# First layer norm of a fused attention and feed-forward kernel: two statistics split into tasks, the first transposed tile copied out by two engines, and another written-out order

## The chip, the cores and the metric

The kernel runs on one core of a Trainium2 chip. The metric is the device time of one launch in microseconds (us). Five engines work side by side: TensorE (PE: matmuls, with its weight loads shown as PEld), VectorE (DVE), ScalarE (ACT), GpSimd (POOL) and SyncE (SP, which here only issues transfers). Each engine takes its instructions in the order in which they stand in its queue; what crosses engines is tied by semaphores.

## The reference, cut to what matters

```
xn  = (x - mean(x)) / sqrt(var(x) + 1e-5)          # x: 2048 x 512, per row
q, k, v = xn @ wq, xn @ wk, xn @ wv                # 32 heads of 16
for s in 4 segments of 512 rows:
    p      = softmax(q_s k_s^T / 4 + mask)         # causal inside the segment
    a_dot  = p v_s
    a_mem  = phi(q_s) M / (phi(q_s) z + 1e-6)      # phi(t) = t+1 if t>0 else exp(t)
    o_s    = g * a_mem + (1 - g) * a_dot           # g = sigmoid(beta), per head
    M, z  += phi(k_s)^T v_s, sum phi(k_s)
out = x + o @ wo + silu(xn @ w1) @ w2              # w1: 512 x 1792, w2: 1792 x 512
```

Inputs and output are bf16. The layer norm is needed by every product, so nothing but warm-up matmuls can run on PE before the first rows are normed.

## The kernel before, in words

The 2048 rows are 16 tiles of 128 rows, four tiles to a segment. The layer norm of a segment (function `ln`) works tile by tile: DVE takes statistics (`bn_stats`, then `bn_aggr`, line 583 and 584; in segment 0 also an addition of epsilon, line 586), POOL raises the variance to the power -1/2 (`rstd`, lines 596 and 606), DVE norms (`xn`, line 617). In segments 1 to 3 the normed tile is transposed by a transfer (`xnT`, line 651, issued on SP). In segment 0 PE transposes it against an identity into a PSUM bank (`tr`, line 630) and one engine copies the bank out into `xnT` (line 643 on ACT for tiles 0 to 2, line 645 on DVE for tile 3). Tile 2 of segment 0 has its statistics on ACT instead.

From the four transposed tiles PE makes keys and queries in blocks of eight heads (four units `u` to a segment), values, and the feed-forward's hidden tiles (`h`: a matmul group, then a tanh on ACT at line 1174 and a product on DVE at line 1178, `glu`). For the very first unit keys and queries are made in pieces: `k0` for tile 0, for tile 1, and for tiles 2 and 3 together, and `q0` the same. A product of scores `S` (line 504, into the four PSUM banks `psS`) is followed by an exponential on ACT (line 870, 1.88 us each, 72 of them) and two causal masks on POOL (line 889). `PV` multiplies the probabilities with the values into two PSUM banks, which DVE copies out into `N` and `O` (line 958). PE has four banks `ps` beside `psS`; a group that finds none free waits for the copy that frees one. One constant is worked out on the way: the heads' gate `gcol` from a load of `beta` (`bet`, 128 partitions x 64 bytes), which the attention's end in segment 0 needs first.

No queue is left to chance. The program first makes some 1700 tasks, each with its engine and its instructions, and then emits them in the sequence of `ORDER`, a list of task numbers written into the file; that list alone says how tasks follow each other on each engine. Buffers are handed out in the same sequence. A task's own waits are those of its data and buffers only: the planner's durations and due times that stand beside the tasks set nothing on the chip.

At the head of the program SP and ACT issue the loads: the four tiles of segment 0, then `w_v`, half of `w_k`, half of `w_q` (ACT), half of `w_1`, tiles 4 to 7, and the other halves. Before that data is there PE runs 52 small matmuls on the identity (`warm`).

Of the kernel before, what the change touches and what calls it, by code (L numbers as in the profile page):

```python
# [10 lines left out]
BF16 = mybir.dt.bfloat16  # L11
# [3 lines left out]
P = 128  # L15
S = 2048
D = 512
# [47 lines left out]
1 3 5 6 14 27 0 53 28 29 17 15 54 2 30 31 32 63 33 34 35 36 58 37 38 18 39 40 41 55 4 64 65  # L65
42 43 44 45 46 47 48 59 60 56 7 49 50 51 61 70 52 66 67 57 114 71 115 62 116 117 68 69 97 72
8 118 96 73 74 109 100 16 98 110 111 9 101 102 104 10 11 99 103 112 113 105 119 21 120 121
122 184 185 136 137 268 138 269 139 270 123 271 26 75 76 77 304 305 188 272 84 129 130 131
132 189 187 140 143 106 141 306 12 13 273 307 147 148 133 149 150 192 193 124 125 126 127 151
107 78 79 80 142 274 128 152 83 195 275 308 153 276 108 85 86 154 196 197 309 89 179 180 181  # L70
182 191 277 198 278 155 156 163 164 279 165 166 167 200 201 194 186 286 287 288 289 183 290
87 280 281 135 282 283 291 134 298 299 203 204 202 81 168 169 170 171 292 88 172 284 199 190
205 206 300 301 293 294 295 302 285 208 303 296 158 220 144 209 210 159 160 207 297 328 346
347 222 348 349 350 212 213 221 82 310 311 312 329 313 330 90 363 364 365 366 351 145 146 314
331 161 162 367 315 332 174 157 333 91 211 19 216 433 20 434 435 436 437 316 317 318 319 382
383 384 217 219 368 385 386 214 226 352 353 443 444 445 215 446 447 322 320 321 323 324 325
354 369 218 227 230 175 173 326 355 390 391 327 392 393 176 356 357 223 394 396 224 231 234
358 428 429 225 430 431 359 360 361 387 677 678 679 680 177 178 432 420 421 235 238 422 423
424 334 335 336 337 681 239 229 371 682 372 373 374 242 340 395 338 409 410 411 412 339 237
341 241 233 236 438 375 342 240 243 245 343 344 244 439 228 413 388 92 246 247 451 452 453  # L80
454 455 456 457 458 459 460 461 462 463 464 465 466 440 232 441 401 248 345 415 22 442 402
403 250 517 467 518 404 405 378 379 93 519 94 579 468 520 262 251 254 406 263 521 264 252 580
253 689 425 690 691 692 522 255 380 256 257 426 572 362 249 671 672 673 571 674 693 258 694
407 259 675 676 523 524 525 526 527 528 261 529 530 531 487 488 260 587 381 683 389 489 490
491 492 493 370 494 495 581 582 585 586 408 573 574 588 496 591 583 265 684 685 377 686 497
416 23 592 595 267 498 687 707 266 708 376 709 710 688 502 503 589 448 450 596 504 593 711
712 598 597 505 506 599 507 508 499 532 427 533 509 510 500 577 511 501 469 512 600 603 872
513 24 594 590 397 604 449 701 534 702 470 601 703 704 705 873 575 706 584 535 514 607 515
516 536 471 537 538 602 606 605 623 476 25 477 578 624 608 625 475 611 417 612 614 613 539
540 541 542 713 714 715 716 576 841 842 473 717 718 615 616 1115 874 1116 843 875 844 845  # L90
1117 1118 1119 609 610 474 755 756 757 617 758 759 619 620 543 544 545 785 719 720 786 721
722 478 876 629 1120 546 723 1103 1104 724 787 788 472 725 877 726 483 1105 789 727 1106 618
728 622 630 633 1107 485 621 626 486 479 480 1108 398 399 737 634 627 738 739 761 740 484 637
481 635 846 847 848 628 731 732 733 734 878 883 729 730 636 849 482 547 632 548 414 638 640
641 850 549 741 735 736 418 760 742 885 565 566 550 551 567 568 400 553 554 555 419 556 569
642 884 645 644 762 695 696 793 794 795 796 697 797 646 647 648 790 698 812 552 813 649 557
814 815 831 631 643 816 832 650 881 833 834 835 699 700 639 559 560 561 562 563 763 764 653
654 766 767 886 768 769 819 665 666 657 836 837 838 770 839 743 652 744 95 658 1006 745 746
840 747 748 879 749 750 661 662 751 774 775 998 791 776 777 778 804 667 805 656 752 660 806
753 807 655 820 754 798 1013 823 824 663 825 826 827 808 913 659 914 915 958 959 1005 960  # L100
1014 1017 1018 997 651 664 668 670 669 817 780 1016 961 962 851 963 779 964 887 1133 1007
1008 1009 1010 999 1021 1022 1000 1134 1097 792 1098 1099 888 880 1100 1003 1011 893 1135
1136 1137 916 917 918 1025 1026 1138 1024 965 966 967 1019 1012 968 852 919 1101 854 855 856
857 858 859 860 861 862 863 864 865 866 867 868 869 1029 1015 920 921 922 870 928 929 821 923
924 1001 1023 818 889 894 969 1028 930 931 765 1027 1102 1030 1033 1034 970 925 971 932 926
892 933 934 935 936 1031 937 1037 1032 938 939 927 1020 1109 1110 1111 972 1112 1038 891 1004
1113 1049 1041 940 1114 895 941 1002 1050 1127 1128 1051 1129 1130 942 799 896 882 1035 1188
1036 1189 1190 1191 558 781 1042 1039 1131 890 782 783 1045 1196 1197 1132 1044 1198 1199 897
1151 1200 1152 1153 1040 1043 1154 1181 1182 1183 1184 1046 1192 898 1055 1241 1155 1156 1185
899 1047 1242 1243 1244 1048 900 1056 1201 1052 1059 901 1245 902 1053 903 564 784 904 909  # L110
809 1246 1247 1248 1249 943 1251 771 1250 905 1060 828 944 1187 945 1252 772 1202 1063 810
946 1054 947 1121 1186 1122 1123 906 1124 822 1064 1125 1256 1257 1258 1259 1062 1061 910
1260 811 1067 1126 948 1253 1254 1203 1204 1205 1206 1207 1065 1255 949 950 951 1068 1071 829
1057 830 952 953 853 907 908 1211 1212 954 955 956 1213 911 773 912 1072 1075 1282 1283 1214
1284 1208 1218 1219 1220 1221 1058 1222 1070 1073 1285 800 1226 1215 1227 1228 1229 957 1076
1079 1139 1140 1141 1066 1069 1230 1142 1074 1091 801 802 1080 1092 1143 1083 1084 1157 1158
1159 1160 570 1082 973 974 975 976 1161 1077 1093 1286 1145 1146 1087 1209 977 1088 1162 1147
1287 1148 991 992 1144 993 994 871 1232 985 986 1288 1295 987 988 989 990 1149 1150 1407 1408
1085 995 1163 1164 1165 1166 1233 1234 1235 1289 1167 1291 1236 979 980 1411 1412 981 1168
982 1237 983 803 1169 1170 1171 1172 1086 1078 1090 1173 1089 1410 1193 1081 1094 1095 1216  # L120
1096 1415 1175 1409 1176 1296 1177 1523 1178 1524 1525 1526 1290 1264 1265 1266 1416 1297
1267 1268 1269 1419 1270 1174 1210 1179 1493 1180 1494 1271 1298 1299 1495 1420 1496 1272
1194 1497 1262 1498 1273 1417 1413 1261 1274 1414 1275 1276 1277 1418 1217 1278 1279 1353
1354 1355 1303 1302 1423 1280 1195 1356 1293 1357 1358 1424 1359 1360 1304 1305 1306 1426
1338 1339 1340 1361 1527 1528 1362 1427 1511 1512 1513 1514 1428 1363 1341 1342 1422 1301
1343 1344 1515 1421 1345 1431 1432 1346 1364 1430 1311 1365 1516 1347 1300 1366 1425 1443
1367 1445 1435 1436 1517 1518 1519 1520 1315 1348 1444 1349 1292 1323 1521 1434 1294 1324
1312 1307 1433 1325 1326 1522 1437 1439 1440 1327 1328 1329 1313 1350 1308 1351 1429 1223
1316 1309 1438 1352 1314 1442 1441 1330 1263 1331 1332 1310 1238 1449 1450 1451 1333 1317
1318 1319 996 1334 1335 1336 978 1337 1446 1447 1448 1239 1240 1320 1453 1454 1368 1452 1456  # L130
1535 1536 1537 1499 1500 1501 1502 1503 1538 1539 1231 1540 1224 1369 1370 1457 1321 1371
1372 1373 1374 1504 1553 1554 1555 1375 1225 1556 1458 1461 1462 1577 1322 1578 1579 1459
1455 1383 1384 1460 1385 1557 1463 1386 1387 1464 1505 1506 1507 1580 1508 1465 1466 1376
1377 1395 1396 1397 1509 1398 1378 1399 1379 1380 1558 1381 1469 1470 1510 1541 1468 1542
1543 1467 1382 1544 1485 1473 1388 1545 1559 1581 1486 1560 1561 1562 1582 1583 1529 1530
1531 1532 1487 1474 1476 1592 1593 1563 1389 1390 1400 1475 1477 1546 1590 1564 1533 1594
1534 1281 1571 1572 1573 1574 1586 1595 1391 1392 1471 1393 1394 1478 1401 1547 1548 1588
1549 1480 1550 1402 1575 1551 1481 1482 1565 1403 1552 1479 1472 1591 1483 1484 1576 1566
1567 1568 1569 1657 1584 1599 1600 1404 1405 1658 1659 1660 1621 1622 1639 1614 1623 1624
# [113 lines left out]
def kernel(  # L253
# [292 lines left out]
    def ln(s, due):  # L546
        first = s == 0
        for js in LNG if first else ((0, 1), (2, 3)):
            ag = []
            for j in js:  # L550
# [41 lines left out]
                if first and j == STJ:  # L592
                    ag[-1].ready = STR
# [819 lines left out]
```

## Time and profile before

| what | value |
|---|---|
| median of 13 runs | 228.8 us (227.71 to 230.65) |
| profiled execution | 229.2 us, of which the profile's span is 227.5 us |
| PE busy | 218.5 us (96%), 2800 matmuls |
| ACT, DVE, POOL busy | 181.5, 172.6, 160.9 us |
| first half of `w_k` used by PE | from 9.92 us |
| first half of `w_q` used by PE | from 12.51 us |
| first exponential starts | 16.91 us |
| mean granted PE clock | 0.992 |

The span runs from the first instruction to the last; the 1.7 us between it and the profiled execution's own time lie around it. Busy times are unions of an engine's instructions. In the timeline a row gives the start, the length, the engine, the line, the operation with output and input, how many instructions are merged, and in brackets the idle time before and what ended it.

### The profile page before, as it was taken

Reading aid. Unit: us, or ns where it says so; the run is one execution under the profiler, and the core shown is the slowest. Engines: PE = TensorE matmul, PEld = TensorE weight load, DVE = VectorE, ACT = ScalarE, POOL = GpSimd, SP = SyncE. Lnnn points to the kernel's source line nnn. Section 1 sums busy time; section 2 is a strip of 40 time slices with the busy share of each in tenths; the row PEclk is TensorE's granted clock in tenths of the full one; section 3 lists DMA queues with packets and bytes.
Section 4 is the critical chain, followed back from the end, with each engine's and each line's share of the span. In section 5 each row is a group of like instructions: output and inputs, shape, how many; then the busy total and the mean of one; then the engine's idle time right before and its main releaser. Section 6 shows DMA issues by size and latency. Waiting matters only on the chain.

```text
span 227.5 us, 6765 instructions
## 1 busy us (share of the span) xinstructions
PE 218.5 (96%) x2800; PEld 104.0 (46%) x2800; DVE 172.6 (76%) x307; ACT 181.5 (80%) x166; POOL 160.9 (71%) x281
## 2 busy tenths in 40 slices
PE   7689999999998999999999999999999999999994
PEld 7444444354543353534444445435454544445553
DVE  3649889687798667888897599898656697676883
ACT  4339999999998989999978889889998798994200
POOL 3705678999999756779899777866985976469300
PEclk9969999999999999999999999999999999999999
DMA  6980462708414532143026642001406220123402
GB/s 176 356 256 0 94 121 33 179 6 261 133 23 96 102 71 82 62 105 125 1 57 134 77 139 63 0 12 43 118 15 159 87 70 0 50 65 113 129 8 92
DMA packets 30851, 21.10 MB, mean 93 GB/s; under 512 B 15972, under 2 KB 29924, under 8 KB 30820
## 3 DMA queue, kind: packets, MB, share of 16 engines
q1 hardware_dynamic: 29476, 19.88, 33.8%
q10 hardware_dynamic: 1344, 0.79, 1.1%
q8 instruction: 22, 0.36, 0.7%
q14 instruction: 9, 0.07, 0.1%
HBM read 11.73 MB, written 2.64 MB: 63 GB/s over the span
## 4 chain that ended last, share of the span: by engine, by line
PE 77%; DVE 6%; POOL 5%; DMA 5%; ACT 3%; issue 2%; ACTq 1%; POOLq 0%
PE ps L504 65%; PE psS L504 12%; DMA w_q<-in_A_wq_dram 5%; ACT Pt L870 2%; POOL Pt L889 2%; DVE xn L617 2%; POOL rstd L606 1%; POOL kB L747 1%; DVE hT L1178 1%; POOL pq L675 1%; DVE st L583 1%; DVE O L958 1%; DVE pq L681 1%; DVE kT L742 1%; POOL rstd L596 0%
## 5 line engine op out<-in xcount | busy, mean ns | idle before, releaser
L870 ACT ACTIVATE Pt<-psS 128x2048 bf16<-128x2048 f32 x72 | 135.2, 1877 | 17.0 <-PE psS L504 14.9
L889 POOL TENSOR_SCALAR_AFFINE_SELECT Pt<-Pt 64x512 bf16<-64x512 bf16 (+1 forms) x144 | 89.2, 628 | 27.0 <-ACT Pt L870 22.0
L504 PE MATMUL ps<-xnT,w 128*128 128x512 bf16 x224 | 59.5, 380 | 1.3 <-DVE O L958 0.8
L504 PE MATMUL ps<-w,hT 128*128 128x512 bf16 (+1 forms) x210 | 52.9, 366 | 0.0
L1178 DVE SCALAR_TENSOR_TENSOR hT<-hT,ps 128x512 bf16<-128x512 bf16 x56 | 37.3, 678 | 15.7 <-ACT hT L1174 15.3
L1174 ACT ACTIVATE hT<-ps 128x512 bf16<-128x512 f32 x56 | 32.6, 596 | 0.5 <-PE ps L504 0.2
L504 PEld LDWEIGHTS <-hT 128*128 128x128 bf16 x238 | 21.7, 98 | 23.9 <-issue 3.1
L504 PEld LDWEIGHTS <-w 128*128 128x128 bf16 x224 | 20.4, 98 | 25.3 <-issue 3.8
L504 PE MATMUL psS<-qT,kB 32*128 32x256 bf16 (+5 forms) x640 | 28.6, 261 | 0.1
L504 PEld LDWEIGHTS <-kB 32*128 32x128 bf16 x640 | 11.8, 92 | 26.3 <-issue 24.2
L747 POOL TENSOR_SCALAR kB<-kT,pm 128x512 bf16<-128x512 bf16 x30 | 22.3, 749 | 0.9
L504 PE MATMUL ps<-xnT,w_q 128*128 128x512 bf16 (+2 forms) x72 | 18.2, 372 | 1.7 <-DMA w_q<-in_A_wq_dram 1.7
L504 PE MATMUL ps<-xnT,w_k 128*128 128x512 bf16 (+2 forms) x72 | 18.6, 364 | 1.2 <-DMA w_k<-in_A_wk_dram 1.2
L504 PE MATMUL ps<-Pt,V 64*32 64x256 bf16 (+5 forms) x640 | 19.8, 260 | 0.0
L504 PE MATMUL ps<-Pt,VS 64*32 64x256 bf16 (+5 forms) x640 | 18.7, 261 | 0.0
L504 PE MATMUL ps<-w_v,xnT 128*128 128x512 bf16 x64 | 18.2, 390 | 0.3 <-DMA w_v<-in_A_wv_dram 0.3
L504 PEld LDWEIGHTS <-V 64*32 64x32 bf16 x640 | 14.2, 91 | 8.3 <-issue 3.6
L504 PE MATMUL ps<-w_o,N 128*128 128x512 bf16 (+1 forms) x57 | 14.8, 368 | 0.0
L807 DVE CAST V<-ps 128x512 bf16<-128x512 f32 x16 | 11.0, 685 | 4.5 <-PE ps L504 4.2
L1080 POOL TENSOR_TENSOR pq<-pq,Dr 128x512 bf16<-128x512 bf16 x12 | 14.2, 1189 | 0.2
L583 DVE BATCH_NORM_STATS2 st<-x_all 128x6 f32<-128x512 bf16 x15 | 10.2, 679 | 4.3 <-DMA x_all<-in_A_x_dram 4.3
L504 PEld LDWEIGHTS <-VS 64*32 64x32 bf16 x640 | 12.8, 91 | 0.2
(105 smaller groups left out, 254.5 us busy)
## 6 DMA issues: line engine op xcount, KB each, us to landing
w<-in_B_w_dram SPq DMA_DIRECT2D x4, 896.0 KB
VS<-V SPq DMA_DIRECT2D x8, 264.0 KB
R<-dR SPq DMA_DIRECT2D x15, 128.0 KB
out_dram<-o_t SPq DMA_DIRECT2D x15, 128.0 KB
Dr<-dE SPq DMA_DIRECT2D x12, 128.0 KB
x_all<-in_A_x_dram SPq DMA_DIRECT2D x2, 512.0 KB
N<-O SPq DMA_DIRECT2D x12, 64.0 KB
w_v<-in_A_wv_dram SPq DMA_DIRECT2D x1, 512.0 KB
```

The lines of the kernel that those rows point to most:

```text
L504: nc.tensor.matmul(o, lhsT=l, rhs=r, start=start, stop=stop, **k)
L583: nc.vector.bn_stats(out=b.tile[:], in_=xt(t))
L606: nc.gpsimd.tensor_tensor(out=rs, in0=mv[:, t : t + n, 1:2] if first else rs, in1=lnc[:, 0:n, 1:2], op=ALU.pow,)
L617: nc.vector.tensor_scalar(out=xb.tile[:], in0=xt(t), scalar1=mv[:, t, 0:1], scalar2=rstd[:, t, 0:1], op0=ALU.subtract, op1=ALU.mult,)
L675: nc.gpsimd.tensor_scalar(out=dst_b.tile[:], in0=dst_b.tile[:], scalar1=1.0, scalar2=0.0, op0=ALU.min, op1=ALU.max,)
L747: nc.gpsimd.tensor_scalar(out=kB[u].tile[:, :, KB * r : KB * r + KB], in0=kT[u].tile[:].rearrange("p (a b) -> p a b", b=KB), scalar1=pm[:, ...
L807: nc.vector.tensor_copy(out=bass_pair(o), in_=i)
L870: nc.scalar.activation(out=pb.tile[:], in_=psS[:], func=AF.Exp, scale=SCALE)
L889: nc.gpsimd.affine_select(out=v, in_=v, compare_op=ALU.is_ge, fill=0.0, base=0, pattern=pat, channel_multiplier=-1,)
L1080: nc.gpsimd.tensor_tensor(out=pb.tile[:], in0=pb.tile[:], in1=rb.tile[:], op=ALU.mult)
L1174: nc.scalar.activation(out=hb.tile[:], in_=b.tile[:], func=AF.Tanh, scale=0.5)
L1178: nc.vector.scalar_tensor_tensor(out=hb.tile[:], in0=hb.tile[:], scalar=1.0, in1=b.tile[:], op0=ALU.add, op1=ALU.mult)
```

## The change

It has three parts in the code and one in the list.

1. The statistics of tiles 1 and 3 of segment 0 are two tasks instead of one: `bn_stats`, and then `bn_aggr` with the addition of epsilon. The instructions are the same.
2. The transposed tile 0 is copied out of its bank by ACT (two of four column blocks) and DVE (the other two). All products of segment 0 that read a transposed tile through `first_tile` or `v_tile` also wait for that second half.
3. `ORDER` is another list, for 1724 tasks in place of 1721.

```
-ORDER = """ 1 3 5 6 14 27 0 53 28 29 17 15 54 2 30 31 ...   (1721 numbers)
+ORDER = """ 1 3 5 6 0 53 15 2 65 14 27 28 29 30 31 32 ...   (1724 numbers)
...
+    extra = []
...
-                def f_st(t=t, b=b, vj=vj):
+                cut = first and j in (1, 3)
+
+                def f_st(t=t, b=b):
                     nc.vector.bn_stats(out=b.tile[:], in_=xt(t))
+
+                def f_ag(t=t, b=b, vj=vj):
                     nc.vector.bn_aggr(out=mv[:, t, :], in_=b.tile[:])
                     if first:
                         nc.vector.tensor_scalar(
                             out=vj, in0=vj, scalar1=EPS, scalar2=None, op0=ALU.add
                         )
...
-                    eng = "DVE" if j == 3 else "ACT"
...
+                    parts_ = (("ACT", 0, 2), ("DVE", 2, 2)) if j == 0 else (
+                        ("DVE" if j == 3 else "ACT", 0, 4),)
+                    for eng, lo, n_ in parts_:
+                        def f_e(j=j, pb=pb, eng=eng, lo=lo, n_=n_):
+                            o = xnT_b[0].tile[:, lo : lo + n_, j * P : (j + 1) * P]
+                            i = pb.tile[:].bitcast(BF16)[:, lo * P : (lo + n_) * P].rearrange(
+                                "p (a b) -> p a b", a=n_)
...
-            pcs.append(A("PE", ..., [xnT_done[0][j] for j in js] + [loads],
+            pcs.append(A("PE", ..., [xnT_done[0][j] for j in js] + extra + [loads],
...
-                     lambda ki: w_v[:, ki, :], (xnT_done[s] if s else [xnT_done[0][j]]) + [ld_v], ...
+                     lambda ki: w_v[:, ki, :], (xnT_done[s] if s else [xnT_done[0][j]] + extra) + [ld_v], ...
```

The new list changes the sequence on every engine but ACT's transfer queue, from the first POOL instruction to the last transfer. The stretches that the prediction speaks of, with the tiles' numbers (`v00` is the values of tile 0, `N3` and `O3` are the copies of line 958 for unit 3, `rstd 8,9` the two POOL instructions for tiles 8 and 9; "tiles 8 to 11" is one load):

| queue, stretch | before | changed |
|---|---|---|
| PE, head | 22 warm pairs, tr0, 3 warm, tr1, 1 warm, v00, tr2, k0 tile 1, k0 tile 0, tr3, q0 tile 0, q0 tile 1, k0 tiles 2-3, q0 tiles 2-3, v01, S0 | 20 warm pairs, tr0, 2 warm, tr1, 2 warm, k0 tile 0, v00, tr2, k0 tile 1, 1 warm, tr3, 1 warm, q0 tile 0, q0 tile 1, q0 tiles 2-3, a quarter of v03, k0 tiles 2-3, S0 |
| DVE, head | statistics 0, 1, xn0, xn1, statistics 3, xn2, xn3, V0, xnT3 | statistics 0, 1 (both tasks), xn0, xn1, half of xnT0, statistics 3 (both tasks), xn2, xn3, kT, xnT3 |
| DVE, norm of tiles 8-11 | statistics 10, 11, 9, 8, then two glu, acc, phi, phi, xn11, phi, xn10, gsum, O3, N3 | statistics 9, 8, 10, phi, xn8, xn9, glu, M32, statistics 11, acc, phi, O3, N3, gcol, phi, phi, xn10 |
| DVE, norm of tiles 12-15 | statistics, O7, N7, xn14, phi, xn13, xn15 | statistics 15, qT, glu, xn14, xn15, glu, O7, N7, phi, xn13 |
| SP, after the head | xnT4, phiK, VS, VS, xnT6, xnT5, xnT7, phiK, phiK, half of w_2, phiK (unit 3), half of w_2, w_o, tiles 8 to 11 | xnT4, VS, VS, phiK, xnT6, xnT7, `bet`, xnT5, phiK, phiK, phiK (unit 3), both halves of w_2, w_o, tiles 8 to 11 |
| SP, load of `bet` | last of the loads at the head | see the row above |
| DVE, end | the copy `mem` (line 1242) stands ahead of the last unit's PV copies | `mem` stands right ahead of the two `tailA` (lines 1260 and 1264) |

## Prediction

> **What bounds the kernel now.** I read the page first, then PE's waits, then the head in the windows view, then the two stretches where PE waits, in the timeline. The page says that PE has work nearly all the time, and that its clock is lowered once, near the start:
>
> ```profile
> PE 218.5 (96%) x2800; PEld 104.0 (46%) x2800; DVE 172.6 (76%) x307; ACT 181.5 (80%) x166; POOL 160.9 (71%) x281
> ...
> PEclk9969999999999999999999999999999999999999
> ```
>
> Busy matmul rows can hide bubbles, so I checked the spacing: eight matmuls of 512 columns take 1.89 us in one row, and one alone shows 0.38, so (1.89 - 0.38) / 7 = 0.216 us from start to start, with no room in it. The waits of PE between 16 and 224 us name only three:
>
> ```profile
> PE ps L504 <- DVE O L958: 0.8, 1, 0.8
> PE ps L504 <- DVE hT L1178: 0.3, 1, 0.3
> PE ps L504 <- DVE kT L742: 0.2, 1, 0.2
> ```
>
> So from the moment PE has its operands the time is PE's work plus small holes. Moving a PE task earlier or later gains nothing in itself. Only three things can change the time: when dense work starts, at which clock it runs, and the holes. The head, as rows of the windows view (PE busy second, granted clock second from the right of the engines):
>
> ```profile
> 5.84:9.26 3.42, 2.60 (x29) 1.71 (x26) 2.63 (x9) 1.66 (x3) 2.21 (x13) 1.00 1.04 362
> 9.26:12.67 3.41, 1.00 (x15) 0.84 (x16) 0.93 (x3) 0.58 (x2) 2.33 (x13) 1.00 1.10 362
> 12.67:16.08 3.41, 3.41 (x19) 2.22 (x18) 1.63 (x4) 1.38 (x3) 0.00 (x0) 0.50 0.94 276
> ```
>
> After a stretch with 1.00 us of work PE gets half its clock for 3.41 us, just when it is dense: 1.7 us lost. What it was short of is in the timeline, weights:
>
> ```profile
> 7.49 1.02 PE L504 MATMUL ps<-w_v,xnT 128*128 128x512 bf16 x4 [0.30 <-DMA w_v<-in_A_wv_dram]
> ...
> 9.92 0.62 PE L504 MATMUL ps<-xnT,w_k 128*128 128x128 bf16 x8 [1.18 <-DMA w_k<-in_A_wk_dram]
> ...
> 12.51 0.93 PE L504 MATMUL ps<-xnT,w_q 128*128 128x128 bf16 x8 [1.74 <-DMA w_q<-in_A_wq_dram]
> ```
>
> The holes of 0.3 and 0.8 us lie in the norm of tiles 8 to 11. DVE waits for those tiles' load, then for POOL's `rstd`, and the copy that frees PE's bank stands behind the `xn`:
>
> ```profile
> 59.39 0.69 DVE L583 BATCH_NORM_STATS2 st<-x_all 128x6 f32<-128x512 bf16 x1 [0.95 <-DMA x_all<-in_A_x_dram]
> ...
> 68.55 0.41 DVE L617 TENSOR_SCALAR xn<-x_all,mv,rstd 128x512 bf16<-128x512 bf16 x1 [0.60 <-POOL rstd L606]
> ...
> 70.42 0.68 DVE L958 CAST O<-ps 128x512 bf16<-128x512 f32 x1
> ```
>
> [...]
>
> **The change part by part**, against the profiled execution (229.2 us; it is 0.4 above the median of 228.8, so its loss of clock is somewhat above the usual one).
>
> *Split statistics.* The second task stands directly behind the first on DVE for tile 1 and tile 3. The same instructions come in the same sequence: 0.
>
> *Copy of tile 0 in two halves.* ACT's copy is 0.6 us (1.31 for two). Its half should take 0.37, as line 779's copy of 256 columns, and DVE's half at most 0.42, which is what the row of 512 columns at line 645 took. DVE does it after xn1 (ends 6.62), so tile 0 is whole at 6.9 to 7.1 instead of 7.0. Nobody can use the gain: PE's next task is then `k0` of tile 0, which waits for `w_k` until 9.92. DVE's statistics of tile 3 slip by up to 0.42; its transpose ran only at 10.38, although xn3 ended at 8.84, 1.5 us of cover. 0, from -0.1 to +0.1.
>
> *PE's head.* `k0` of tile 0 now stands ahead of v00 and tr2, so PE idles from about 7.2 (end of tr1 and its warm pairs) to 9.92. Between 9.92 and 12.51 it must then do v00 (4 x 0.216 = 0.86), eight small `k0` (8 x 0.056 = 0.45, 128 of 512 columns being a quarter of 0.216), two transposed tiles (8 x 0.056 = 0.45) and two warm pairs (0.22): 2.0 us in 2.6, so at full clock nothing slips past 12.51. All that stood ahead of `w_q` before still does.
>
> *Clock.* The new hole moves the poor stretch forward. In 5.84 to 9.26 PE would hold some 16 to 20 small matmuls, about 1.3 us of busy rows, as poor as the 1.00 that brought on half clock. With the same phase the slow 3.41 us would then be 9.26 to 12.67[...]. Of the 2.0 us of work 1.4 is done by 12.67 (2.75 us at half rate), the rest by 13.3: 0.8 lost in place of 1.7. I take -0.9 in this phase. Ends: -1.7 (not lowered) and 0 (the phase puts the slow stretch behind 12.5 as now). Against the median I count half, -0.45.
>
> *Norm of tiles 8 to 11.* The load of these tiles is issued behind the unit-3 transpose and three weight loads, as before. But that transpose and both halves of w_2 now come in one run, some 5 us earlier, and after it nothing on SP waits: 2.8 MB at the 360 to 389 GB/s seen at 54 to 58 us is 7.7 us, so it lands before the 58.4 us at which DVE wanted it (it landed at 59.4). The wait of 0.95 goes. And O3 and N3 stand ahead of xn10, behind xn8 and xn9 alone. PE's two holes are 0.38 + 0.93 = 1.3 us from start to start, above the usual spacing. Late next is xn8: its `rstd` stands behind a POOL that is 13.14 of 14.2 us busy, and a wait like the present 0.60 would leave about 0.3 at PE. So -1.0; ends -1.3 and +0.5.
>
> *Norm of tiles 12 to 15.* Here the sequence goes the other way. O7 and N7 now stand behind xn14 and xn15, which wait for POOL. The wait before that xn was 0.41 and cost PE nothing, as the copies were done. It can reach PE now, less DVE's gaps: +0.2, from 0 to +1.2.
>
> *`bet`.* Its issue held SP for 1.60 us behind the head's loads; now it holds SP between xnT7 and xnT5. The last of these transposes landed at 36.38, and PE's first product on it ran at 36.6. An issue with no backlog ahead took 0.37 (second half of `w_q`), which fits within a tenth or two of that slack: 0, from 0 to +1.2 should it hold SP for 1.6 again. Queued behind it are xnT5 and the `phiK` transposes; only xnT5 has PE waiting. `gcol`, which needs `bet`, is first used at 80.96 (line 1122), over 40 us later.
>
> *End.* `mem` (0.69) enters the DVE chain from 211.76 to 220.32, which has only 0.27 idle. But behind the last `tailA` PE then has 22 matmuls, 18 of them of 256 columns (2.9 us) where it had 27 (3.9): 0, from -0.2 to +0.6. POOL's constants come earlier or later in time that POOL had free at the head: 0.
>
> Sum: -0.9 - 1.0 + 0.2 = -1.7 from 229.2 gives **227.5 us**; from the median with the half count, 228.8 - 0.45 - 0.8 = 227.55.
>
> **The rivals.** A measurement of this kernel can tell about 0.5%, 1.1 us, from no change.
>
> *The holes only move* (same). PE holds the same work in both; a list of 1724 tasks with POOL this full has its own waits. If the 1.0 comes back elsewhere and the clock gives half, 228.8 - 0.45 = 228.3. For it: the three waits before are all of one kind, a bank freed late. Against it: the load's wait of 0.95 has a plain cause that goes.
>
> *Slower: POOL's `rstd` ahead of O7 and N7.* If POOL works off four masks (2.35 us in one row at 111.56) and a `pq` product (1.15) before rstd 14,15, DVE stands still up to 3.5 us, and PE with four banks follows after about two groups (8 x 0.216 = 1.7): +1.8, and with nothing saved elsewhere 230.6. It decides from a wait of about 2 us at that xn. For it: these are POOL's fullest stretches. Against it: the same wait was 0.41.
>
> *The clock doesn't follow the head.* [...]if the typical launch is not slowed before, the -0.45 is 0 and the rest gives 228.0. It lies inside "same".
>
> **How the numbers follow.** Faster 0.46 (the sum; 226.3 to 227.6), same 0.32 (holes move, or clock unchanged), slower 0.22 (rival two, or another list wait of that size). The likeliest is 227.5. The range takes the better clock end (227.5 - 0.8 - 0.4 = 226.3) and the slower case (230.6): 226.2 to 230.6.
>
> **What would show it.** Right: v00 starts behind 9.92; the half-clock stretch is earlier or gone; no DVE wait for `x_all` near 58; no PE wait for O3. Wrong: half clock still behind 12.5, PE waits for DVE `N` or `O` near 117 to 121, or a new PE wait for `xnT` near 36.

## The result and the profile after

The changed kernel takes 232.18 us (median of 11 runs, 231.14 to 234.6) against 228.71 us (48 runs) of the kernel before: 1.0155 times as long, interval 1.0127 to 1.0184. The profiled execution took 231.96 us, 230.1 of them its span (229.2 and 227.5 before). The forecast was 227.5, with a range of 226.2 to 230.6; the measured time lies outside it, on the slower side. Ratios here leave out disturbed runs and those over 1.5% above a kernel's fastest, among them some with a stretch of half clock (5 of e15's 22 runs), so that a ratio can be smaller than the quotient of two medians.

The page of the changed kernel, the lines that answer to those shown of before (busy time; granted clock in 40 slices):

```profile
PE 219.4 (95%) x2800; PEld 104.5 (45%) x2800; DVE 179.4 (78%) x308; ACT 181.1 (79%) x166; POOL 161.6 (70%) x281
...
PEclk9979999999999999999999999999999999999999
```

PE does the same work, again with one dip of the clock. DVE, whose instructions are the same but for the copy in halves, is busy for 6.8 us more: some of them became longer. PE's waits between 16 and 224 us (total, times, longest):

```profile
PE ps L505 <- DVE hT L1203: 1.4, 1, 1.4
PE ps L505 <- DMA VS<-V: 0.8, 1, 0.8
PE ps L505 <- DVE N L1184: 0.6, 1, 0.6
PE ps L505 <- DMA xnT<-xn: 0.5, 1, 0.5
PE psS L505 <- ACT Pt L895: 0.3, 1, 0.3
PE ps L505 <- DVE V L832: 0.2, 1, 0.2
PE ps L505 <- DVE acc L1228: 0.2, 1, 0.2
```

Seven waits stand where before had three. Those of before (0.8 for O, 0.3, 0.2) are gone. From start to start, above the spacing that matmuls of that shape usually have, the large new ones are 0.66 us at 35.5, 1.14 at 129.5, 1.56 at 142.3 and 0.80 at 219.6. Together they are 4.2 us, and the two holes that went were 1.3 by the prediction's count: +2.9, about the 2.6 by which the two spans differ. Both profiled executions had one stretch of half clock (granted clocks 0.992 and 0.993), so the clock has little part in this difference. The head, as rows of the windows view (PE busy second, granted clock third from the end of the row):

```profile
5.84:9.26 3.42, 1.67 (x17) 1.33 (x16) 2.37 (x9) 0.96 (x2) 1.91 (x7) 1.00 1.08 370
9.26:12.67 3.41, 2.98 (x23) 2.26 (x24) 0.65 (x2) 0.59 (x1) 1.33 (x9) 0.68 1.09 353
12.67:16.08 3.41, 3.41 (x28) 2.23 (x26) 2.32 (x5) 1.20 (x3) 0.00 (x0) 0.82 1.02 307
```

The half-clock stretch moved forward, as forecast: the two last clocks are 0.68 and 0.82 instead of 1.00 and 0.50 (it lies from 10.46 to 13.87). What stands ahead of it in PE's timeline is one long hole before `k0` of tile 0. By `q0` nothing has to be waited for:

```profile
9.69 0.40 PE L505 MATMUL ps<-xnT,w_k 128*128 128x128 bf16 x4 [2.18 <-DMA w_k<-in_A_wk_dram]
...
12.80 1.56 PE L505 MATMUL ps<-xnT,w_q 128*128 128x128 bf16 x12
```

In the norm of tiles 8 to 11 DVE's timeline shows no wait: statistics, then `xn` (two in one row), and O3, N3 ahead of xn10:

```profile
60.89 0.68 DVE L587 BATCH_NORM_STATS2 st<-x_all 128x6 f32<-128x512 bf16 x1
...
63.88 1.22 DVE L632 TENSOR_SCALAR xn<-x_all,mv,rstd 128x512 bf16<-128x512 bf16 x2
...
68.19 0.69 DVE L983 CAST O<-ps 128x512 bf16<-128x512 f32 x1
68.79 0.68 DVE L983 CAST N<-ps 128x512 bf16<-128x512 f32 x1
```

So far the profile says what the prediction said. The largest part of the loss lies behind 128 us. First wait, 129.5: the PV product needs two pieces of the values with their heads swapped (`VS`, a transfer). SP issued them 3.5 us apart (start, length of the issue):

```profile
123.07 0.55 SPq L844 DMA_DIRECT2D VS<-V  x1
123.72 1.45 SPq L1131 DMA_DIRECT2D Zg<-dZ  x1
125.22 0.59 SPq L1137 DMA_DIRECT2D N<-O  x1
125.90 0.65 SPq L1098 DMA_DIRECT2D Dr<-dE  x1
126.61 0.51 SPq L844 DMA_DIRECT2D VS<-V  x1
```

and PE's PV starts, then stops until the second has landed:

```profile
130.71 0.37 PE L505 MATMUL ps<-Pt,VS 64*32 64x448 bf16 x4 [0.78 <-DMA VS<-V]
```

Second wait, 142.3: DVE's three products of `N` with the broadcast reciprocals `R` (line 1169; called a_t below) stand ahead of the `glu` that frees PE's bank. DVE:

```profile
140.14 3.29 DVE L1169 TENSOR_TENSOR N<-N,R 128x512 bf16<-128x512 bf16 x3
143.35 0.68 DVE L1203 SCALAR_TENSOR_TENSOR hT<-hT,ps 128x512 bf16<-128x512 bf16 x1
```

POOL beside it:

```profile
139.32 1.15 POOL L1105 TENSOR_TENSOR pq<-pq,Dr 128x512 bf16<-128x512 bf16 x1
140.42 0.60 POOL L914 TENSOR_SCALAR_AFFINE_SELECT Pt<-Pt 64x256 bf16<-64x256 bf16 x1
141.01 1.35 POOL L772 TENSOR_SCALAR kB<-kT,pm 128x512 bf16<-128x512 bf16 x2
```

and PE:

```profile
144.08 0.81 PE L505 MATMUL ps<-w_v,xnT 128*128 128x512 bf16 x3 [1.39 <-DVE hT L1203]
```

The three took 0.61, 1.96 and 0.87 us. Of the 15 products of this kind in this profile, the five with no POOL instruction beside them took 0.41 to 0.43 us; of the ten that POOL overlapped, nine took 0.57 to 1.96 and one 0.42. In the profile of before six of the ten that POOL overlapped took 0.51 to 0.87, four 0.42 to 0.43. The one of 1.96 us, started at 140.68, ends 0.3 us after POOL's second `kB`. No run took POOL's work away from beside them, so that POOL is what lengthens them is argued from these durations; that their place costs PE its wait is what e7 and e15 test.

### The profile page after: what moved, and what is told of

Read it like the earlier page. It is cut to its first block, busy times and chain, and to the rows that moved or that the text cites. A ratio compares the mean times of both kernels' runs of the same rounds, so it can differ in the third digit from the quotient of the medians.

```text
span 230.1 us, 6776 instructions
## 1 busy us (share of the span) xinstructions
PE 219.4 (95%) x2800; PEld 104.5 (45%) x2800; DVE 179.4 (78%) x308; ACT 181.1 (79%) x166; POOL 161.6 (70%) x281
## 4 chain that ended last, share of the span: by engine, by line
PE 67%; DVE 12%; DMA 9%; ACT 5%; POOL 4%; issue 1%; SPq 1%; ACTq 0%; DVEq 0%; POOLq 0%
PE ps L505 57%; PE psS L505 9%; ACT Pt L895 4%; DMA w_k<-in_A_wk_dram 3%; DMA xnT<-xn 2%; DVE hT L1203 2%; DVE st L587 2%; DMA VS<-V 2%; DVE N L1169 1%; DMA R<-dR 1%; DVE xn L632 1%; DVE pkT L706 1%; POOL Pt L914 1%; POOL Mbf L1022 1%; POOL pq L1105 1%
## 5 line engine op out<-in xcount | busy, mean ns | idle before, releaser
L914 POOL TENSOR_SCALAR_AFFINE_SELECT Pt<-Pt 64x512 bf16<-64x512 bf16 (+1 forms) x144 | 91.3, 641 | 31.4 <-ACT Pt L895 24.8
L505 PE MATMUL ps<-xnT,w 128*128 128x512 bf16 x224 | 60.2, 380 | 0.3 <-DVE V L832 0.2
L505 PEld LDWEIGHTS <-w 128*128 128x128 bf16 x224 | 19.9, 98 | 25.0 <-issue 5.1
L772 POOL TENSOR_SCALAR kB<-kT,pm 128x512 bf16<-128x512 bf16 x30 | 21.6, 725 | 2.1 <-ACT hT L1199 1.2
L983 DVE CAST N<-ps 128x512 bf16<-128x512 f32 x15 | 10.3, 684 | 5.7 <-PE ps L505 5.7
L983 DVE CAST O<-ps 128x512 bf16<-128x512 f32 x15 | 10.2, 682 | 3.5 <-PE ps L505 3.5
```

What stands on the lines that cost most here:

```text
L505: nc.tensor.matmul(o, lhsT=l, rhs=r, start=start, stop=stop, **k)
L772: nc.gpsimd.tensor_scalar(out=kB[u].tile[:, :, KB * r : KB * r + KB], in0=kT[u].tile[:].rearrange("p (a b) -> p a b", b=KB), scalar1=pm[:, ...
L914: nc.gpsimd.affine_select(out=v, in_=v, compare_op=ALU.is_ge, fill=0.0, base=0, pattern=pat, channel_multiplier=-1,)
L983: nc.vector.tensor_copy(out=dst.tile[:, dt, :], in_=buf.tile[:])
```

## The experiments

Each run gives its mean granted clock. One stretch of 3.41 us at half clock in 230 us lowers it by 0.5 x 3.41 / 230 = 0.0074, to 0.993. The last columns use that: how many runs were below 0.995, counted here as runs with at least one such stretch (the profiles of before and changed, with one each, have 0.992 and 0.993), and the median span of the others. The changed kernel has a clock on record for 12 runs.

| kernel | us | ratio to before, interval | below 0.995 | span of the others |
|---|---|---|---|---|
| before, four sets | 228.25, 228.36, 228.2, 229.0 | 1 | 2 of 25, 8 of 26, 12 of 50, 26 of 67 | 226.5, 226.3, 226.2, 226.7 |
| changed | 232.18 | 1.0155 (1.0127 to 1.0184) | 10 of 12 | 229.4 |
| e1, swap moved | 232.11 | 1.0167 (1.0129 to 1.0204) | 4 of 4 | |
| e2, edits on the old list | 228.31 | 0.9996 (0.9971 to 1.002) | 1 of 14 | 226.4 |
| e3, head of the new list | 229.39 | 1.0051 (1.0025 to 1.0077) | 8 of 12 | 227.4 |
| e4, first half of the new list | 234.65 | 1.0299 (1.0252 to 1.0345) | 4 of 4 | |
| e5, end of the old list | 234.42 | 1.0241 (1.0183 to 1.0298) | 4 of 4 | |
| e6, k0 behind v00 | 231.29 | 1.0118 (1.0075 to 1.016) | 1 of 6 | 229.2 |
| e7, e1 and a_t moved | 230.99 | 1.0104 (1.0045 to 1.0163) | 2 of 4 | 227.8 |
| e9, e7 with k0 and `bet` moved | 229.3 | 1.0041 (1.0016 to 1.0066) | 10 of 21 | 227.1 |
| e10, head's hole filled | 231.56 | 1.0152 (1.0106 to 1.0198) | 3 of 6 | 228.7 |
| e11, before with one move | 227.5 | 0.9969 (0.9946 to 0.9992) | 6 of 22 | 225.5 |
| e12, before with three repairs | 228.58 | 1.0006 (0.9983 to 1.003) | 5 of 22 | 226.0 |
| e13, e9, a_t again, holes filled | 228.14 | 0.9997 (0.9976 to 1.0019) | 0 of 14 | 226.2 |
| e14, e11 with two holes filled | 229.49 | 0.9996 (0.9973 to 1.0019) | 10 of 22 | 227.2 |
| e15, swap and a_t moved | 230.86 | 1.0036 (1.0004 to 1.0067) | 14 of 22 | 227.4 |
| e16, e15 with the hole filled | 229.06 | 0.9983 (0.9954 to 1.0012) | 2 of 14 | 227.0 |
| e17, e16 with `bet` at the head | 229.07 | 1.001 (0.9987 to 1.0033) | 0 of 22 | 227.1 |

Sets were taken on different chips (e1 to e4; e5, e6, e7, e9 and e10 to e13; e14 to e17); the ratio is to the kernel before beside each. Edits are shown as pieces of an engine's sequence. Where a run follows one list up to a point and the other list from there, that point is called its seam. In the experiments' profiles the helper of PE is line 502 (501 where the code is that of before).

**e1.** On SP:

```
- VS 5, Z, merge, den, VS 4
+ VS 5, VS 4, Z, merge, den
```

> The changed kernel with one transfer moved: the second values' swap of segment 2 (VS#4) stands on SP right behind the first (VS#5), ahead of a Z transfer, a merge and a den transfer, where the changed list has it behind the three. Theory A (SP's late swap holds PE 1.1 us at 129.5, DVE falls behind by it, and its three a_t products then run into POOL's kB copies and hold PE another 1.5 us at 142.3): both waits go, 232.2 - 2.6 = 229.5 us, ratio to before about 1.003. A with the two waits independent: the 1.14 us wait goes alone, 231.0, ratio 1.010. Theory C (holes only move on a list as crowded as this): less than 0.5 us gained, 231.7 or more, with a wait of about 1 us elsewhere between 125 and 150.

The time stayed, as theory C has it, but with a plain cause. PE's waits of e1 show it:

```profile
PE ps L502 <- DVE hT L1200: 1.8, 1, 1.8
PE ps L502 <- DVE pkT L703: 0.5, 1, 0.5
```

The wait for VS is gone, and the wait for the `glu` grew from 1.4 to 1.8. DVE reached the a_t products 0.9 us earlier (139.26 instead of 140.14), but they took 3.61 us instead of 3.29, so that the `glu` ran at 142.79 instead of 143.35. The second wait is not a consequence of the first, and takes up part of what the first gave. Behind that hole the clock fell a second time:

```profile
144.04:147.45 3.41, 3.41 (x20) 1.05 (x18) 3.30 (x6) 1.00 (x2) 1.22 (x2) 0.50 0.00 0
```

So this hole of 1.8 us cost some 3.5, an estimate: the hole and half of 3.41. Three of the 12 runs of the changed kernel have clocks of 0.978 to 0.985, as two or three such stretches would give (spans 232.5 to 232.7). Where theirs lay is not shown; four runs of e15, whose profile has no such hole at 142, have 0.985 too.

**e2.** The code of the change, the list of before, each new task right behind its predecessor:

```
  ... statistics 1, + second task, ... statistics 3, + second task, ... xn1, tr0, + half of xnT0 ...
```

> The changed code (statistics as two tasks, the tile copied out by two engines with the wait that the products get) on the list of the kernel before; each new task stands right behind the one that it was part of. Theory A (the list alone costs the time): 228.7 +- 0.4, ratio 0.998 to 1.002. Theory B (the edits cost the time: the copy on DVE, the added wait of the products): most of the 3.5 us, 231 or more, ratio 1.010 or more.

Ratio 0.9996 (0.9971 to 1.002): the edits cost nothing that can be told from the noise. The list does.

**e3** and **e4** follow the new list up to a score product and the old one from there.

```
e3: new list up to S0, then what is left in the old sequence
e4: new list up to S35 (about 108 us), then what is left in the old sequence
```

> The changed list until the first product of scores S0, then the list of the kernel before for everything that is left. Theory A: the head is what the change gains (slow clock moved forward, 0.8 to 0.9 us earlier in its trace at 16 us), and all of the loss comes later: 228.0, between 227.7 and 228.5, ratio about 0.996. Theory B (edits or head cost): 229.5 or more, ratio 1.004 or more. Theory C (holes move): 228.7, the gain of the head eaten within the list.

> The changed list until the score product S35 (about 108 us), then the list before. Theory A: contains the gained head, the wait of 0.66 us for xnT5 at 35.5 and the norm of tiles 8 to 11, and none of the three waits behind 120 us: 228.2 +- 0.5, ratio about 0.998. Theory C: the loss is spread over the whole list, about half of 3.5 us by then: 230 or more, ratio 1.006 or more.

e3 is 0.5% slower instead of 0.3% faster, with 8 of 12 runs below 0.995 where 2 of 25 of before were: the first sign that the new head brings on the slow clock rather than shifts it. Its full-clock span of 227.4 is 0.9 above before's; its profile has a wait of 0.68 us at 18.4, where the changed kernel has 0.42, and one of 0.58 at 60.7 that neither list has, so a part of this is the seam. e4 tells nothing of its question, since the waits for ACT behind its seam are longer than the sought loss:

```profile
PE psS L502 <- ACT Pt L892: 4.6, 3, 3.7
```

**e5** cuts late, at S68. 

```
new list up to S68 (about 200 us), then what is left in the old sequence
```

> The changed list until the score product S68 (about 200 us), then the list before, so the end of the kernel before: the R loads ahead on SP, mem early, the last unit's outputs in the old sequence. If the end's wait of 0.80 us (at 219.6 in the changed kernel's profile, for a bank that DVE frees late because an R load is late) is in every run: 231.4, ratio to before 1.012. If it is in that one profile only (the kernel with the swap moved showed 0.12 there): 232.0 to 232.2, ratio 1.0155. A seam can cost some tenths by itself.

Also hidden by its seam (1.39 us at 206 and 0.82 at 203 from start to start). What sets the changed kernel's wait at its end stays open: it was 0.80 us in the changed kernel's profile, 1.07 in e6, 1.28 in e7, 1.01 in e15, 0.69 in e17, but 0.12 in e1 and not to be seen in e9, e13 and e16. A kernel with the R loads ahead of two other transfers there has no run.

**e6** and **e7** take one place each.

```
e6, PE:  - tr1, 2 warm, k0 tile 0, v00, tr2     + tr1, 2 warm, v00, k0 tile 0, tr2
e7, DVE (on top of e1):
  - acc, a_t, a_t, a_t, glu, N, acc, O, V
  + acc, glu, a_t, N, a_t, acc, O, a_t, V
```

> The changed kernel with k0 of tile 0 moved on PE from ahead of v00 to behind it: one PE group in the head, nothing else. Theory D (the hole that k0 of tile 0 opens at 7.2 to 9.7 makes the slow clock the rule: 11 of 12 runs of the changed kernel have granted clocks under 1 and 10 of them 0.993 or less, where the kernel before had 3 of 25 under 0.998; one slow stretch costs about 1 us by the spans): most runs at 0.998 or more, 231.3, ratio 1.011 to 1.013. If the clock is not set by that hole: the same clocks as the changed kernel, 232.1, ratio 1.0155 or more.

> The kernel with the swap moved (e1), and on DVE the three a_t products of 139 to 143 us put behind the glu and the PV copies that free PE's banks (sequence acc, glu, a_t, N, a_t, acc, O, a_t), no other engine changed. Theory E (they take 3.3 to 3.6 us instead of 1.2 because POOL is busy beside them, and PE's bank waits behind them, whatever the swap does; the hole of 2 us sometimes brings a second slow stretch of the clock of 1.5 us): PE's wait at 141 to 142 is under 0.4, span at clock 0.993 about 227.9, 229.8 us, ratio 1.004 to 1.009. If the bank was late for another reason (PV, the score banks): still 1.5 to 2 us at 141, 231.9, ratio 1.015.

e6 came out as theory D says, in clocks and in time, but with six runs, and its ratio is not clear of the changed kernel's. e7's median is 1.1 us below e1's, with four runs each and intervals that overlap. Its profile shows the effect better: the wait of 2.0 us becomes 0.58 and 0.38 at 142.9 and 145.3, since an a_t still stands ahead of a copy.

**e9** adds up e7, e6 and `bet`'s load at the head.

> All together on the changed list: the swap moved, the a_t products behind the glu, k0 of tile 0 behind v00, and bet's load back behind the last weight load at the head. Theory (each cause is separate and its size adds): from 232.2: swap 1.1, a_t 1.6, clock 0.9, bet 0.5 (0.66 at 35.5 less what else holds xnT5): 228.1, ratio to before 0.998, between 0.995 and 1.003. If the holes only move: 229.5 or more, ratio over 1.005.

Of 3.5 us, 1.0 is left (ratio 1.0041). But 10 of 21 runs were below 0.995, with the same PE head as e6's 1 of 6. So e6's clocks were in part luck: the two holes left there (1.7 us ahead of v00, 1.6 ahead of `q0` in e9's profile) are enough. So the next step was to fill holes rather than to move what stands in them.

**e10, e13.** Fill with warm-up matmuls on the identity; e13 also takes the remaining a_t products from the banks' way.

```
-        def f_w():
-            for _ in range(2):
+        def f_w(i=i):
+            for _ in range({23: 36}.get(i, 2)):        # e10, e16, e17;  e13: {23: 26, 25: 28}
e13, DVE: + acc, glu, a_t, N, acc, O, V, oT, a_t, a_t, phi, glu
```

> The changed kernel with PE's hole in the head filled: the last pair of warm-up matmuls ahead of k0 of tile 0 becomes 36 matmuls (about 2.0 us at 0.056 each), list and everything else as changed. Theory D (the hole, not the position of k0, brings on the slow clock): nearly all runs at a granted clock of 0.998 or more where 10 of 12 of the changed kernel were at 0.993 or less, time 231.2, ratio to before 1.010 to 1.013 (the later waits stay, and can still bring a slow stretch behind 142). If the clock comes from something else in the head: clocks and time as in the changed kernel, 232.1, ratio 1.0155 or more.

> The four repairs of e9 on the changed list, with DVE's sequence at 138 to 146 us once more changed (acc, glu, a_t, N, acc, O, V, oT, a_t, a_t, so that no bank waits behind an a_t but one) and the head's holes filled with 26 and 28 warm-up matmuls. Theory D and E: e9 was 229.3 with 10 of 21 runs in a slow stretch and 0.8 + 0.4 us of PE waits at 141 and 144; without both 228.0, ratio 0.995 to 1.001, clocks 0.998 or more. If the rest of e9's loss lies elsewhere in the list: 229.2, ratio 1.004.

e10 alone is unclear: 3 of 6 runs below 0.995, at spans of 230.3 to 230.9 against 227.8 to 228.8, and the hole of 142 was still in it (1.97 us at 140.0 in its profile). In that profile no 3.41 us of the head, wherever one lets them begin, have PE busy for less than 3.0 us, but those around the later hole come down to 1.6. So the three may have got their half clock there; no trace shows it. e13 is the repaired change: all 14 runs at 0.999 or more, ratio 0.9997.

**e15 to e17** take e13 apart.

```
e15: changed list, VS as in e1, DVE's sequence at 138 to 146 us as in e13
e16: e15 with the hole ahead of k0 filled (36 matmuls)      e17: e16 with bet's load at the head
```

> The changed list with the two moves of the middle alone (the swap moved; DVE's sequence of e13 at 138 to 146 us); head, bet and end as changed. Theory D: the middle's 2.7 us go, the head's slow stretch stays in most runs (0.993): 229.4, ratio 1.004 to 1.007. Otherwise, if the slow stretches of the changed kernel came from the hole at 142: clocks of 0.998 or more in most runs, 228.6.

> The same, with the hole ahead of k0 filled with 36 warm-up matmuls; k0 of tile 0 stays ahead of v00. Theory D (the hole and not k0's position): all runs at 0.998 or more, 0.8 below e15, 228.5, ratio 1.000 to 1.003. If the position of k0 matters in itself: as e15.

> The same as e16, with bet's load back behind the last weight load at the head. Theory (bet's issue is why xnT5 is late at 35.5): PE's wait there falls from 0.4 to 0.66 to under 0.2, time 0.4 below e16, 228.1. If xnT5 is late by the transposes alone: the wait stays, no difference to e16.

e15, DVE: the `glu` now runs ahead of the a_t, and two of these have slipped to where PE's waits behind DVE are short (0.22 us at 146.06 and 0.33 at 147.00):

```profile
138.31 0.68 DVE L1200 SCALAR_TENSOR_TENSOR hT<-hT,ps 128x512 bf16<-128x512 bf16 x1
138.90 1.02 DVE L1166 TENSOR_TENSOR N<-N,R 128x512 bf16<-128x512 bf16 x1
...
143.21 1.60 DVE L1166 TENSOR_TENSOR N<-N,R 128x512 bf16<-128x512 bf16 x2
```

The two moves take the ratio from 1.0155 to 1.0036, some 2.7 us, and the full-clock span from 229.4 to 227.4; 14 of 22 runs stay below 0.995. e16 differs in the head's hole alone, with `k0` still ahead of v00. Its PE timeline and windows:

```profile
7.26 2.29 PE L502 MATMUL psS<-ident 128*128 128x128 bf16 x38
9.39 0.39 PE L502 MATMUL ps<-xnT,w_k 128*128 128x128 bf16 x4
```

```profile
5.84:9.26 3.42, 3.22 (x49) 2.96 (x49) 2.38 (x9) 0.96 (x2) 1.97 (x5) 1.00 1.07 354
9.26:12.67 3.41, 3.28 (x41) 2.53 (x40) 2.01 (x6) 0.80 (x2) 1.52 (x10) 1.00 1.10 362
12.67:16.08 3.41, 3.10 (x19) 1.38 (x18) 2.27 (x6) 2.25 (x4) 0.00 (x0) 1.00 0.79 232
```

Only 2 of 14 runs remain below 0.995, the median falls from 230.86 to 229.06, and the ratio is 0.9983. The hole decides how often the clock falls, and not where `k0` stands. e17 equals e16 within its interval: `bet` between the transposes costs nothing that shows, against the theory that it makes xnT5 late. None of e17's 22 runs is below 0.995.

**e11, e12, e14** try single moves on the kernel before.

```
e11, DVE:  - xn11, phi, xn10, gsum, O3, N3     + xn11, phi, O3, N3, xn10, gsum
e12: e11; one statistics of tiles 8, 9 behind the two glu; warm-up {24: 20} behind tr2, {25: 28} behind tr3
e14: e11 and e12's warm-up alone
```

> The kernel before with one of the change's moves alone: on DVE xn10 and gsum behind O3 and N3 (in the norm of tiles 8 to 11). Theory (PE's wait of 0.93 us at 70.0 is a real part of the time, and the prediction's step of -1.0 was right in kind): that wait is under 0.3, 227.6, ratio 0.996 to 0.998. If holes only move: the wait comes back within the next 10 us or at the end, ratio 0.999 to 1.001.

> The kernel before with three repairs: xn10 and gsum behind O3 and N3; one statistics (tile 8 or 9) behind the two glu that free PE's banks at 64.5 (wait of 0.65 us); and the head's two holes filled with 20 and 28 warm-up matmuls ahead of k0 and of q0. Theory: 0.9 + 0.5 from the two waits, and 0.2 from the runs (10 of 51 of the kernel before on these chips) that had a slow stretch: 227.0, ratio 0.992 to 0.996; granted clock 0.998 or more in all runs. If holes only move: 228.2, ratio 0.999.

> The kernel before with xn10 and gsum behind O3 and N3 (e11) and the head's two holes filled with 20 and 28 warm-up matmuls; the statistics stay where they were, which e12 moved. Theory D: e11's 0.7 us stay, and the slow stretch that 6 of e11's 22 runs had is gone (all at 0.998 or more): 227.2, ratio 0.993 to 0.997. If e12's slow runs came from the filled head and not from its moved statistics (its profile has a wait of 1.7 us for an exponential at 99 instead): some runs at 0.993 again and 228 or more.

e11's DVE copies O3 out 0.9 us behind the start of the `xn` of tile 11, where before took 1.9:

```profile
67.15 0.41 DVE L614 TENSOR_SCALAR xn<-x_all,mv,rstd 128x512 bf16<-128x512 bf16 x1 [0.60 <-POOL rstd L603]
67.48 0.68 DVE L678 SCALAR_TENSOR_TENSOR pq<-qT,pq 128x512 bf16<-128x512 bf16 x1
68.08 0.68 DVE L955 CAST O<-ps 128x512 bf16<-128x512 f32 x1
```

PE's wait at 70 is gone and time with it: ratio 0.9969, full-clock spans 0.7 shorter (its profile has a new wait of 0.97 at 155). e11 is the one version that beats both kernels: 227.5 us. e12 lost this again; its profile shows a wait of 1.68 us for an exponential at 99. The moved statistics or the fill may have brought it; no run tells which. e14's profile has its hole of 1.5 us ahead of v00 (`w_v` late, and two warm-up pairs fewer ahead of it), and 10 of 22 runs below 0.995: two of three holes filled were not enough. Its ratio, 0.9996, doesn't show e11's gain, and a kernel before with all three holes filled has no run.

## Why the prediction was wrong, point by point

*Split statistics, copy in halves: 0.* Right (e2).

*PE's head.* Right that everything of the head still fits ahead of `q0`. (A quarter of its 0.216 is 0.054 and not 0.056; nothing hangs on it.) The term put the price of a PE hole at its own length; the price lay in the clock.

*Clock: -0.45 against the median.* The step that failed first. How the clock follows PE's work the prediction could read from one stretch in the trace of before (0.50 behind 1.00 us of work); the rest was the author's estimate. Right was that the slow stretch moves forward. The gain of it was small: by the matmuls started, each weighted with its usual spacing, the changed kernel's profile is 0.9 us ahead of before's at 17 us, but only 0.2 from 22 to 34. And counting half of a gain for the median took the profile of before, at 0.992, for about as common as a launch without a slow stretch. By the table 48 of its 168 runs had one, with median spans 0.6 to 1.2 us above the others', so that even to end them all would give only some 0.2 to 0.3 us in the mean (an estimate from these numbers). Of the changed kernel's runs 10 of 12 had one, and 14 of 22 of e15, which has the changed head, beside 26 of 67 of before in that set. The hole of 2.18 us made the rule what was the exception. The term's ends, -1.7 and 0, left no room for that, nor did the third rival. From e15 to e16, where only the hole goes, this term measures +1.8 us at the median (1.2 by the ratios), with the opposite sign.

*Norm of tiles 8 to 11: -1.0.* Right in kind, the load's wait and both holes went; e11 gives it as -0.7 by itself. In the changed kernel five waits of 0.27 to 0.66 us between 17 and 118 us (2.1 together) took the place of before's three (2.0), so nothing of it reached the end.

*Norm of tiles 12 to 15: +0.2.* About right: 0.27 at 117.3. The slower rival, POOL's `rstd` ahead of O7 and N7, did not happen.

*`bet`: 0.* Held in time (e16, e17). PE's wait of 0.66 for xnT5 at 35.5, named as a sign of wrong, is there, but the issue of `bet` took 0.57 us; xnT5 landed 4.7 us behind its own issue in the changed kernel and 4.5 in e15, where PE waits, and 2.8 in e16, where it doesn't. The profile of e10, too, has `bet` in this place and no such wait, so `bet` alone is not its cause; why the landing varies stays open.

*End: 0, up to +0.6.* 0.80 in the profile, but not by `mem`: the a_t of the last segment waits for an R load. Open, as said.

*What the sum left out.* The largest part has no term: 1.14 + 1.56 us at 129 and 142. The prediction followed the stretches where before had waits, and the heads of the queues, and gave the rest of a wholly new list nothing, as if a stretch without waits could only stay so. The rival "the holes only move" had that thought and priced it at the 1.0 that it saw go. This is the second step that failed. The evidence was in reach: SP's and DVE's new sequences show VS 4 behind three transfers and three a_t ahead of a `glu`, and the trace of before had one a_t at 0.87 us beside POOL and another at 0.41 without. At full clock the changed kernel is 229.4 - 226.4 = 3.0 us longer (two of its runs were at full clock), and the clock adds the rest. The two moves of e15 leave 0.7 of it (227.4 beside 226.7), and with the head filled too (e13, e16) the time equals before's.

## What to carry to other kernels

When a list of tasks is replaced as a whole, look for new waits where the old profile has none: go through each queue for what now stands ahead of the instruction that frees a full engine's buffer, and ask how long it becomes beside its neighbours (here 0.41 us alone, up to 1.96 beside POOL). A hole in PE's work is priced with its clock (filling the one in the head took 1.8 us off the median, e15 to e16), and one profile doesn't tell how often the slow stretch occurs; the granted clocks of all runs do. Single moves can be measured: the one good move of this list (PV copies ahead of a late `xn`) gave 0.3% alone, and was lost inside the whole.

## What the runs showed of the hardware

PE had work in each stretch ahead of the half clock (in the heads 1.00 to 1.72 us of 3.41). Each trace keeps the times at which the clock changed. In the head it first becomes full between 4.2 and 7.5 us, at a time that differs among the 18 profiles (5.84 in before, 7.05 in the changed kernel; small matmuls then come every 0.056 us instead of every 0.107), and the later falls lie whole multiples of 3.41 us behind that time (two in before, from 5.84 to 12.67; one in the changed kernel, from 7.05 to 10.46). So the falls came at different times from launch to launch; the prediction had no trace that showed this. Cut into stretches of 3.41 us from that time, the heads sort by how long PE is busy. Behind each stretch with 1.00 to 1.72 us the clock was half: 1.00 (before), 1.06 (e5), 1.23 (changed), 1.35 (e2), 1.36 (e7), 1.38 (e1), 1.42 (e3), 1.56 (e6) and 1.72 (e14). Behind each with 1.92 (e11) or more it stayed full. The changed kernel and e15 have the same head. In the first's profile PE waits 2.18 us for `w_k`, in e15's, where that load came earlier, 1.16 (and 2.75 in e5's, with this head too). So in these profiles the fall hangs on when the load came as well as on where the stretches lie:

```profile
7.05:10.46 3.41, 1.23 (x15) 0.82 (x13) 1.92 (x6) 0.59 (x1) 1.95 (x10) 1.00 1.08 363
10.46:13.87 3.41, 3.41 (x28) 2.86 (x26) 1.24 (x3) 0.62 (x2) 0.28 (x2) 0.50 1.08 365
```

```profile
7.29:10.70 3.41, 2.20 (x28) 1.60 (x27) 1.96 (x7) 0.85 (x2) 1.95 (x10) 1.00 1.08 351
10.70:14.11 3.41, 2.54 (x29) 1.65 (x27) 2.53 (x6) 1.17 (x3) 0.27 (x2) 1.00 1.09 360
```

Later in the kernel busy time alone doesn't sort them: around the hole at 142 half clock came behind a stretch with 1.58 us (e1), but not behind stretches with 1.73 (e5) and 1.79 (e10).

And an a_t product on DVE, 0.41 to 0.43 us alone, took up to 1.96 us beside POOL (at 140.68 in the changed kernel). At 183 us another took 1.95; there PE waits for nothing and it costs nothing.
